# The end of the last block of a state-space and expert kernel: another order of the sums, and the last result accumulated on transposed sums in halves

## The chip, the cores and the metric

One Trainium2 chip, one core. The metric is the device time of one execution in microseconds (us): 611.15 is the median of three runs of the kernel before (610.99 to 611.33). Engines are named as the profile names them: PE is TensorE (PEld its weight loads), DVE is VectorE, ACT is ScalarE, POOL is GpSimd, SP is SyncE, which issues the DMAs here. A bank is one of the eight 128x512 fp32 accumulators of PSUM, the memory that PE writes.

## The reference

A chunked state-space block makes 3072 rows of 256 values; every row then goes through four experts, and the four outputs are added with the row's normalised weights. The change touches only the end of the second part:

```
p = domain_probs / (domain_probs.sum(-1, keepdims=True) + 1e-09)
out = zeros((3072, 256))
for e in range(4):
    h = maximum(x @ w1[e], 0.0)          # w1[e]: 256 x 1024
    out += p[:, e:e + 1] * (h @ w2[e])   # w2[e]: 1024 x 256
```

Everything is fp32.

## The kernel before

**Blocks and units.** The 3072 tokens are worked on in four blocks of six chunks of 128 tokens, that is three pairs of 256 tokens. Each block passes over the 16 slices of 256 hidden features in units of four slices, one expert to a unit. A unit has first products (w1; `fours_first`), gating on DVE, and second products (w2; `second`).

**Products.** In place of the 24 products that a unit's block matrices (w2 cut in four by two, tokens in three pairs) would take one by one, a fast scheme (`G`) takes 20, numbered 0 to 19. Their operands are sums of weight tiles on one side and sums of gated activations (`fours_right`, made by DVE) on the other. One product of the second kind multiplies a 256x128 weight by 256x256 activations: two fp32 matmuls of 128x128 by 128x256, which the profile shows as four matmul records and four weight loads. Its output has 128 model features as rows and 256 tokens as columns.

**Accumulators.** The 20 second products go to 16 accumulators of 128x256: twelve take one product each, and (1,6), (5,18), (2,19) and (3,17) take two each. Two accumulators share a bank; such a pair is a house. `visit` makes a house: ACT copies its sums so far from a tile of kind V (128x512, in SBUF) into a bank (`seed`, line 1035), PE adds the products (line 1021), ACT copies the bank back into V (line 1321). A house in `HELD` (last unit only) stays in its bank. `LATE` is the order of the houses in the last unit.

**Results.** `result` adds and subtracts accumulators in pairs of 128x256 on DVE (`sum_`, line 1372; where no operand is in a bank POOL may take it) until six results stand: half d of the model features (0 or 1) by pair n of the tokens (0 to 2). In the last block each result is written to a tile of its own, and `leave_last` takes it out: PE turns it with two 128x128 transposes into a bank (line 1437), DVE or ACT copies the bank to SBUF (line 1442), SP issues one DMA of 128 KB (line 1444). `LAST` is the order of the six results, and `TAILS` says how many second products come behind each one's turn.

**What sets the order.** PE's instructions go in the order of the list `line`, written by the code. All other engines' orders come from a planner (`Plan.run`): it has a cost for every piece of work (a product 0.863 us, a turn 0.35, a sum 0.34), walks through time, and gives each engine that is free the ready piece with the earliest due time (`latest`). The orders are fixed when the program is built; on the chip each engine goes through its queue in that order and waits where an input is not there.

**The end before.** The last unit's second products run in the order of accumulators 7 9, 15 10, 11 13, 4 8, 12 14, 0 16, (1,6) (5,18), (3,17), (2,19); the last two, which share a house, each have a bank of their own (`APART`). Turn (1,0) and turn (0,0) come ahead of (3,17), turn (0,1) ahead of (2,19), turns (1,1), (1,2), (0,2) at the end. Result (0,2) is (2,19) + 13, result (1,2) is (3,17) + 10.

Of the kernel before, what the change touches and what calls it, by code (L numbers as in the profile page):

```python
# [12 lines left out]
P = 128  # L13
# [6 lines left out]
D512, D256 = .60, .34  # L20
# [287 lines left out]
G = Scheme()  # L308
# [18 lines left out]
def house(*accs):  # L327
    return tuple(a if isinstance(a, tuple) else (a,) for a in accs)
# [1 line left out]

G.houses = (house(7, 9), house(15, 10), house((2, 19), (3, 17)), house(11, 13), house(12, 14),
            house(4, 8), house((1, 6), (5, 18)), house(0, 16))
LATE = (house(7, 9), house(15, 10), house(11, 13), house(4, 8), house(12, 14), house(0, 16),
        house((1, 6), (5, 18)), house((2, 19), (3, 17)))
HELD, APART = LATE[-3:], LATE[-1:]
TAILS = 4, 4, 2, 0, 0, 0
LAST = (1, 0), (0, 0), (0, 1), (1, 1), (1, 2), (0, 2)

B = Scheme()
B.rows, B.pairs = 2, 2  # L340
# [20 lines left out]
def kernel(  # L361
# [446 lines left out]
    def dma(fn, n=1, kb=256, **kw):  # L808
        return plan.add({"SP": ISSUE * n}, fn, lag=LANDING + kb / 190, kb=kb, pieces=n, **kw)
# [7 lines left out]
    def on(e):  # L817
        return {"DVE": nc.vector, "POOL": nc.gpsimd}[e]

    def value(kind, **kw):  # L820
        return Value(kind, **kw)
# [217 lines left out]
    def whole(v):  # L1039
        return v.t if v.kind == "bank" else flat(v)  # L1040
# [230 lines left out]
    def fours_right(h):  # L1271

        T = {0: h[0, 0], 3: h[3, 2], 4: h[3, 0], 6: h[0, 1], 7: h[1, 0], 12: h[2, 0], 18: h[2, 1],
             19: h[0, 2]}
        T[5] = combine(h[3, 0], h[3, 1], reuse=False)
        v = combine(h[3, 1], h[0, 1])
        T[8] = combine(v, h[3, 0], reuse=False)
        T[1] = combine(h[1, 1], h[1, 0])
        T[2] = combine(h[1, 0], h[1, 2], reuse=False)
        u = combine(h[1, 2], h[3, 2])  # L1280
        T[9] = combine(u, h[1, 0], reuse=False)
        T[15] = combine(T[1], h[2, 1], reuse=False)
        T[10] = combine(u, T[15])
        T[17] = combine(h[2, 0], h[2, 2], reuse=False)
        w = combine(h[2, 2], h[0, 2])
        T[14] = combine(w, h[2, 0], reuse=False)
        x = combine(h[0, 0], T[8], reuse=False)
        T[16] = combine(x, T[14])
        T[11] = combine(T[9], v, -1, reuse=v)
        T[13] = combine(w, T[15], -1)  # L1290
        return T
# [3 lines left out]
    def visit(k, house, terms, last=False, only=None):  # L1295
# [31 lines left out]
                hold=HOLD)  # L1327
        return seq

    def second(k, key, groups, houses, held=(), put={}):  # L1330

        seq = []
        for house in houses:
            terms = [
                (acc, weights[key, fbs, 2][0][r],
                 lambda r=r, fbs=fbs: weights[key, fbs, 2][1](r), T[r])
                for acc in house for r in put.get(acc, acc) for fbs, T in groups if r in T]
            for only in reversed(house) if house in held and house in APART else (None,):
                if terms:
                    seq += visit(k, house, terms, house in held, only)  # L1340
        return seq

    def plain_first(fb):
# [8 lines left out]
            for i in range(2)]  # L1352
        return seq, gated(b, gate_of(0, fb), 0)

    def result(k):

        scheme = blocks[k].scheme

        def acc(r):
            for house in scheme.houses:  # L1360
                if r in house:
                    v, i = kept.get((k, (r,)), kept.get((k, house))), house.index(r)
                    return v, lambda: whole(v)[:, i * FB:i * FB + FB]

        def piece(v, i):
            return v, lambda: v.t[:, i]

        def sum_(x, y, sign, o):

            vs = dict.fromkeys((x[0], y[0]))  # L1370
            engines = B256 if all(v.kind != "bank" for v in (*vs, o[0])) else {"DVE": D256}
            plan.add(engines, lambda e: (on(e).tensor_add if sign > 0 else on(e).tensor_sub)(  # L1372
                o[1](), x[1](), y[1]()), reads=[v for v in vs if v is not o[0]],
                two=all(v.kind != "bank" for v in vs), writes=[o[0]])

        A = {r[0]: acc(r) for h in scheme.houses for r in h}

        def into(r, x, y, sign=1):
            sum_(x, y, sign, A[r])

        into(9, A[9], A[10])
        into(14, A[14], A[13])
        into(7, A[7], A[9])
        into(7, A[7], A[15])
        into(4, A[4], A[8])
        into(4, A[4], A[9])
        into(4, A[4], A[11], -1)
        into(11, A[11], A[7], -1)
        into(13, A[13], A[7])
        into(12, A[12], A[14])  # L1390
        into(12, A[12], A[15])
        into(10, A[10], A[12])
        into(12, A[12], A[4])
        into(8, A[11], A[8], -1)
        into(8, A[8], A[14], -1)
        into(8, A[8], A[16])
        parts = {(0, 0): (0, 1, 8), (0, 1): (1, -1, 11), (0, 2): (2, 1, 13),
                 (1, 0): (16, -1, 12), (1, 1): (5, 1, 4), (1, 2): (3, 1, 10)}
        if k < len(blocks) - 1:
            for r, sign, x in parts.values():  # L1400
                into(r, A[r], A[x], sign)
            return [A[r][0] for r in (0, 1, 2)]
        O = {}
        for d, n in LAST:
            r, sign, x = parts[d, n]
            O[d, n] = value("V")
            sum_(A[r], A[x], sign, piece(O[d, n], 0))
        return O

    def leave(k, O, due):  # L1410
        for n in range(len(O)):
# [13 lines left out]
                                    in_=v[32 * x:32 * x + 32, d, c % 2 * 4:c % 2 * 4 + 4])  # L1425
                        dma(fn, 2, 150, reads=[ot], due=due)

    def leave_last(k, O, order):
        dst = out.rearrange("(q k p) (d m) -> d k p q m", q=NSEQ, p=P, d=2)
        tails = []  # L1430
        for x, (d, n) in enumerate(order):
            o, t, r = O[d, n], value("bank", fills=False), value("V")
            c = blocks[k].first + 2 * n

            def turn(e, o=o, t=t):
                for i in range(2):
                    nc.tensor.transpose(
                        t.t[:, i * P:i * P + P], o.t[:, 0, i * P:i * P + P], ident[:, 0])

            tails.append(plan.add({"PE": .35}, turn, reads=[o], writes=[t]))  # L1440
            copy = (nc.vector.tensor_copy, nc.scalar.copy)[x % 2]
            plan.add({("DVE", "ACT")[x % 2]: .36}, lambda e, t=t, r=r, copy=copy: copy(
                out=r.t[:, 0], in_=t.t[:, :2 * P]), reads=[t], writes=[r])
            dma(lambda e, c=c, d=d, r=r: nc.sync.dma_start(
                out=dst[d, c // NSEQ][:, c % NSEQ:c % NSEQ + 2],
                in_=r.t[:, 0].rearrange("p (q m) -> p q m", q=2)), kb=128, reads=[r])
        return tails

    def put(*seqs):
# [104 lines left out]
    for u, (k, fbs) in enumerate(units):  # L1556
        of_block = [v for v, (q, _) in enumerate(units) if q == k]
        i = u - of_block[0] + (not k)
        if u + 1 < len(units):
            unit_weights(u + 1)  # L1560
        if u == of_block[0] and k:
            token_sums(k, G, k)
        seq, h = fours_first(k, fbs)
        lead = 0 if u else LEAD
        merged = seq[:lead] + put(behind, seq[lead:])
        ends.append(merged[-1])
        if not u:
            fold()
        if ending is not None:
            leave(*ending, due=lambda n=u + AFTER: ends[min(n, len(ends) - 1)])  # L1570
            ending = None
        final = u == len(units) - 1
        behind = second(k, k, [(fbs, fours_right(h))], LATE if final else G.houses, HELD if final else ())
        if u == of_block[-1] and k < len(blocks) - 1:
            ending = k, result(k)

        at = {}
        if k < len(blocks) - 1:
            for unit, x, what in PAIRS_AT[k > 0]:
                if unit != i:  # L1580
                    continue
                cs = [blocks[k + 1].first + 2 * int(p) + j for p in what[1:] for j in range(2)]
                mark = len(line)
                if what[0] == "s":
                    for c in cs:
                        fetch(c)
                        decays(c)
                    scores(cs)
                else:
                    outputs(cs)  # L1590
                    for c in cs:
                        carry(c)
                at.setdefault(x, []).extend(line[mark:])
                del line[mark:]
        for x, w in enumerate(merged):
            line.extend(at.get(x, []))
            line.append(w)
    O = result(len(blocks) - 1)
    for i, w in enumerate(leave_last(len(blocks) - 1, O, LAST)):
        behind.insert(len(behind) - TAILS[i], w)  # L1600
    line.extend(behind)

    done = plan.run(line, now, {"PE": now, "DVE": now - 2.6, "ACT": now + .9, "POOL": now - 1.6,
# [56 lines left out]
```

## Time and profile before

| | |
|---|---|
| median of three runs | 611.15 us |
| the profiled execution: its time, its span | 612.22 us, 610.5 us |
| PE busy | 603.0 us, 99% of the span, 3385 records |
| DVE busy | 488.3 us, 80% |
| ACT busy | 296.6 us, 49% |
| POOL busy | 153.9 us, 25% |
| PE's share of the chain that ended last | 93% |
| granted clock of TensorE, mean | 0.999 |

The span runs from the first to the last instruction of the core; the execution's time has a little more around it. Busy time counts what an engine works, a matmul's end being modelled, so that the next matmul starts before the one ahead is shown to end: steps on PE are to be read from start to start. "The chain that ended last" is followed back from the last instruction, at each step to what released it. In a line such as `bank<-v,w 128*128 128x256 f32 x16` stand the output, the operands, the stationary tile's shape, the moving operand's shape and the number of records.

### The profile page before, as it was taken

What the parts mean: (1) busy time and instruction counts of PE and PEld (TensorE: products, weight loads), DVE (VectorE), ACT (ScalarE), POOL (GpSimd) and SP (SyncE); (2) the same over time, 40 slices, a digit from 0 to 9 for tenths busy, and PEclk for the clock granted to TensorE, in tenths of its full rate; (3) what the DMA queues carried; (4) which work ended last, traced back from release to release, by engine and by line L of the source; (5) the groups of instructions that cost most, each with busy time, mean ns of one, the idle gap of its engine ahead of it and who ended that gap; (6) DMA issues with size and microseconds to landing.
All of it is one profiled execution on the core that took longest, in us unless ns stands there. A gap on an engine that the chain in (4) does not pass through costs nothing.

```text
span 610.5 us, 10066 instructions
## 1 busy us (share of the span) xinstructions
PE 603.0 (99%) x3385; PEld 514.7 (84%) x3385; DVE 488.3 (80%) x843; ACT 296.6 (49%) x699; POOL 153.9 (25%) x204
## 2 busy tenths in 40 slices
PE   8999999999999999999999999999999999999997
PEld 5778878888888888888888888888888888888885
DVE  7779887999989894877979988396786989575775
ACT  5567465389443328948251334734444142434441
POOL 5656664536452002776200100200000000000000
PEclk9999999999999999999999999999999999999999
DMA  6866669787823239792422325962241332964001
GB/s 209 272 225 203 217 206 316 262 287 265 289 79 112 45 73 346 276 294 105 148 86 87 113 33 158 309 204 82 74 141 67 99 75 52 354 192 131 1 0 53
DMA packets 88548, 99.78 MB, mean 163 GB/s; under 512 B 26916, under 2 KB 54192, under 8 KB 88496
## 3 DMA queue, kind: packets, MB, share of 16 engines
q1 hardware_dynamic: 88340, 99.08, 51.4%
q8 instruction: 27, 0.44, 0.3%
q14 instruction: 25, 0.20, 0.1%
q10 hardware_dynamic: 156, 0.06, 0.0%
HBM read 78.93 MB, written 20.17 MB: 162 GB/s over the span
## 4 chain that ended last, share of the span: by engine, by line
PE 93%; DMA 2%; ACT 2%; DVE 1%; issue 0%; POOL 0%; SPq 0%; ACTq 0%; DVEq 0%; POOLq 0%
PE bank L1021 88%; PE bank L502 2%; PE bank L551 2%; DMA ah<-cum_d 1%; ACT A L561 1%; PE bank L967 1%; DMA ab<-cum_d 1%; PE bank L688 1%; DMA cum_d<-cum 1%; POOL w L1081 0%; ACT v L982 0%; DVE bank L1179 0%; ACT MT L526 0%; DVE LT L519 0%; DVE v L1372 0%
## 5 line engine op out<-in xcount | busy, mean ns | idle before, releaser
L1021 PE MATMUL bank<-v,w 128*128 128x256 f32 x1640 | 385.3, 380 | 0.0
L1021 PEld LDWEIGHTS bank<-v,w 128*128 128x128 f32 x1640 | 310.4, 190 | 45.3 <-issue 2.1
L1021 PE MATMUL bank<-Y,w 128*128 128x256 f32 x692 | 177.5, 381 | 0.8 <-ACT LT L982 0.4
L1021 PEld LDWEIGHTS bank<-Y,w 128*128 128x128 f32 x692 | 130.2, 190 | 22.2 <-issue 1.5
L1321 ACT COPY v<-bank 128x512 f32<-128x512 f32 x106 | 62.1, 585 | 173.9 <-PE bank L1021 172.9
L1048 DVE TENSOR_TENSOR v<-v,v 128x512 f32<-128x512 f32 x174 | 130.2, 760 | 1.3
L1056 DVE SCALAR_TENSOR_TENSOR v<-bank,gate 128x512 f32<-128x512 f32 x143 | 98.1, 686 | 36.2 <-PE bank L1021 32.4
L1081 POOL TENSOR_TENSOR w<-w,w 128x512 f32<-128x512 f32 (+1 forms) x74 | 80.2, 1094 | 55.1 <-DVE v L1048 15.1
L1030 ACT COPY v<-bank 128x512 f32<-128x512 f32 x99 | 57.9, 586 | 49.2 <-PE bank L1021 42.7
L1179 DVE TENSOR_TENSOR bank<-bank,v 128x512 f32<-128x512 f32 x79 | 53.7, 694 | 33.4 <-PE bank L1021 23.7
L1035 ACT COPY bank<-v 128x512 f32<-128x512 f32 x126 | 72.8, 594 | 10.6 <-DVE v L1056 7.3
L1021 PE MATMUL bank<-LT,w 128*128 128x256 f32 x228 | 58.0, 379 | 0.0
L526 ACT ACTIVATE MT<-ab,neg 128x128 f32<-128x128 f32 x160 | 50.3, 391 | 5.1 <-DMA ab<-cum_d 5.1
L1021 PEld LDWEIGHTS bank<-LT,w 128*128 128x128 f32 x228 | 43.2, 190 | 6.1 <-issue 0.3
L536 POOL TENSOR_SCALAR_AFFINE_SELECT MT<-MT 128x512 f32<-128x512 f32 x38 | 25.3, 675 | 74.7 <-ACT MT L526 56.7
L1048 DVE TENSOR_TENSOR v<-bank,v 128x512 f32<-128x512 f32 x29 | 19.9, 687 | 10.4 <-PE bank L1021 8.8
L944 DVE TENSOR_TENSOR MT<-bank,MT 128x512 f32<-128x512 f32 x36 | 22.7, 678 | 0.4 <-PE bank L502 0.4
L1321 ACT COPY LT<-bank 128x512 f32<-128x512 f32 x15 | 8.8, 586 | 27.8 <-PE bank L1021 24.9
L1056 DVE SCALAR_TENSOR_TENSOR v<-v,gate 128x512 f32<-128x512 f32 x29 | 20.3, 701 | 0.4
L1056 DVE SCALAR_TENSOR_TENSOR LT<-bank,gate 128x512 f32<-128x512 f32 x19 | 13.0, 686 | 7.4 <-PE bank L1021 7.0
L1372 DVE TENSOR_TENSOR v<-v,v 128x256 f32<-128x256 f32 x45 | 17.8, 417 | 1.1 <-ACT v L1321 0.7
L1048 DVE TENSOR_TENSOR v<-v,LT 128x512 f32<-128x512 f32 x25 | 16.9, 683 | 0.3
(128 smaller groups left out, 324.5 us busy)
## 6 DMA issues: line engine op xcount, KB each, us to landing
w<-w_d SPq DMA_DIRECT2D x128, 256.0 KB
w<-in_w_dram SPq DMA_DIRECT2D x72, 256.0 KB
w_d<-w SPq DMA_DIRECT2D x64, 256.0 KB
ab<-cum_d SPq DMA_DIRECT2D x20, 512.0 KB
gate<-p_d SPq DMA_DIRECT2D x15, 384.0 KB
xb<-in_xbc_dram SPq DMA_DIRECT2D x17, 192.0 KB
xb<-in_xbc_dram SPq DMA_DIRECT2D x7, 320.0 KB
out_dram<-v SPq DMA_DIRECT2D x112, 16.0 KB
```

What stands on the lines that cost most here:

```text
L526: nc.scalar.activation(out=MT[:, place(c, h), 0:P], in_=ab[:, h * P:h * P + P], func=AF.Exp, bias=neg[:, h % NT, NQ * real(c) + h // NT:NQ ...
L536: nc.gpsimd.affine_select(out=MT[:, h:h + n, 0:P], in_=MT[:, h:h + n, 0:P], compare_op=ALU.is_ge, fill=0.0, base=0, pattern=[[0, n], [1, P ...
L944: nc.vector.tensor_mul(to, g, to)
L1021: nc.tensor.matmul(out=o, lhsT=w[:, j], rhs=x if half is None else x[:, j], start=(start and j == 0), stop=(j == 1), skip_group_check=True)
L1030: act(.5, lambda e: nc.scalar.copy(out=flat(v), in_=bank.t), reads=[bank], writes=[v])
L1035: act(.54 if to - lo > FB else .32, lambda e: nc.scalar.copy(out=bank.t[:, lo:to], in_=flat(v)[:, lo:to]), reads=[v], writes=[bank])
L1048: plan.add(engines, lambda e: (on(e).tensor_add if sign > 0 else on(e).tensor_sub)(flat(v), whole(x), whole(y)), reads=[x, y], writes=[v], ...
L1056: dve(D512, lambda e: nc.vector.scalar_tensor_tensor(out=h.t, in0=whole(x).rearrange("p (j m) -> p j m", j=JJ), scalar=0.0, in1=g.t[:, 2 * ...
L1081: (on(e).tensor_add if sign > 0 else on(e).tensor_sub)(out, x, y)
L1179: dve(D512, lambda e: (nc.vector.tensor_add if sign > 0 else nc.vector.tensor_sub)(to.t, bank.t, whole(x)), reads=[x, bank], writes=[to])
L1321: act(.5, lambda e: nc.scalar.copy(out=flat(v), in_=bank.t), reads=[bank], writes=[v], hold=HOLD)
L1372: plan.add(engines, lambda e: (on(e).tensor_add if sign > 0 else on(e).tensor_sub)(o[1](), x[1](), y[1]()), reads=[v for v in vs if v is n ...
```

## The change

The houses of the last unit run in another order: 7 9, 15 10, 11 13, 4 8, (1,6) (5,18), 12 14, 0 16. The held houses are (1,6) (5,18), then 12 14, then 0 16. `second` and `result` lose what they had for the last unit and the last block, and `leave_last` goes; a new function `last` writes out the end of the last block:

- The sums are written in another order, with other intermediate values (one more tile, `q`). Results (0,1) and (1,1) come first, then (1,0), (0,0), (1,2); each is turned, copied and sent as before (`piece`), the copies alternating between ACT and DVE.
- (3,17) is made alone in half a bank, seeded from V, as before.
- (2,19) is not seeded. DVE adds its sums so far, in V, to accumulator 13; PE turns the two halves of this sum into two banks; and the products 2 and 19 are then added to these banks with the activations as the stationary operand, 128 tokens at a time, and the weights as the moving one: 128 tokens as rows, 128 features as columns. Behind each half comes a copy of 128x128 (ACT for the first, DVE for the second) and a DMA of 64 KB.
- `TAILS` puts turn (0,1) ahead of product 0, (1,1) ahead of 16, (1,0) and the two single transposes ahead of the first half, (0,0) between that half's products, (1,2) ahead of the second half.

```diff
-LATE = (house(7, 9), house(15, 10), house(11, 13), house(4, 8), house(12, 14), house(0, 16),
-        house((1, 6), (5, 18)), house((2, 19), (3, 17)))
-HELD, APART = LATE[-3:], LATE[-1:]
-TAILS = 4, 4, 2, 0, 0, 0
-LAST = (1, 0), (0, 0), (0, 1), (1, 1), (1, 2), (0, 2)
+LATE = (house(7, 9), house(15, 10), house(11, 13), house(4, 8), house((1, 6), (5, 18)),
+        house(12, 14), house(0, 16))
+HELD, APART = LATE[-3:], house((2, 19), (3, 17))
+TAILS = 8, 7, 4, 3, 2, 4, 4
...
-    def leave_last(k, O, order):
+    def last(k, groups):
+
+        seq = second(k, k, groups, LATE, HELD)
+        A = accumulators(k, LATE)
...
+        def turn(o, t, i, at):
+            nc.tensor.transpose(t.t[:, at:at + P], o[1]()[:, i * P:i * P + P], ident[:, 0])
+
+        def send(d, n, r, to):
             c = blocks[k].first + 2 * n
...
+            dma(lambda e: nc.sync.dma_start(
+                out=dst[d, c // NSEQ][:, c % NSEQ + to.start:c % NSEQ + to.stop],
+                in_=r.t[:, 0, to.start * P:to.stop * P].rearrange("p (q m) -> p q m", m=P)),
+                kb=64 * (to.stop - to.start), reads=[r])
+
+        def piece(d, n, x, y, sign):
+            o, t, r = fresh(), value("bank", fills=False), value("V")
+            sum_(x, y, sign, o)
+            tails.append(plan.add({"PE": .35}, lambda e: [turn(o, t, i, i * P) for i in range(2)],
+                                  reads=[o[0]], writes=[t]))
+            x = len(tails) % 2
+            copy = (nc.vector.tensor_copy, nc.scalar.copy)[x]
+            plan.add({("DVE", "ACT")[x]: .36}, lambda e: copy(
                 out=r.t[:, 0], in_=t.t[:, :2 * P]), reads=[t], writes=[r])
+            send(d, n, r, slice(0, 2))
+
+        into(9, 9, 10)
+        into(7, 7, 9)
+        into(7, 7, 15)
+        into(15, 15, 13)
+        into(9, 9, 11, -1)
+        into(11, 11, 7, -1)
+        q = A["q"] = fresh()
+        sum_(A[11], A[13], -1, q)
+        into(13, 13, 7)
+        into(10, 10, 15)
+        into(4, 4, 8)
+        into(4, 4, 9)
+        into(8, "q", 8, -1)
+        into(15, 15, 4)
+        piece(0, 1, A[1], A[11], -1)
+        piece(1, 1, A[5], A[4], 1)
+        into(15, 15, 12)
+        into(15, 15, 14)
+        into(8, 8, 14, -1)
+        piece(1, 0, A[16], A[15], -1)
+        into(8, 8, 16)
+        piece(0, 0, A[0], A[8], 1)
+
+        into(10, 10, 12)
+        into(10, 10, 14)
+        two, three = APART
+        terms = terms_of(k, groups, APART)
+        begun = kept[k, APART]
+        seq += visit(k, APART, terms, True, three)
+        third = kept[k, (three,)]
+        piece(1, 2, (third, lambda: whole(third)[:, FB:]), A[10], 1)
+        o, ends = fresh(), [value("bank", seeded=True) for _ in range(2)]
+        sum_((begun, lambda: flat(begun)[:, :FB]), A[13], 1, o)
+        tails.extend(plan.add({"PE": .2}, lambda e, t=t, i=i: turn(o, t, i, 0), reads=[o[0]], writes=[t])
+                     for i, t in enumerate(ends))
+        for i, t in enumerate(ends):
+            r = value("V")
+            for acc, w, view, x in terms:
...
+                def fn(e, i=i, t=t, view=view, x=x):
+                    for j in range(JJ):
+                        nc.tensor.matmul(
+                            out=t.t[:, :P], lhsT=x.t[:, j, i * P:i * P + P], rhs=view()[:, j],
+                            start=False, stop=j == JJ - 1, skip_group_check=True)
+
+                seq.append(plan.add({"PE": .52}, fn, reads=[w, x], writes=[t]))
+            plan.add({("ACT", "DVE")[i]: .25}, lambda e, i=i, t=t, r=r: (nc.scalar.copy, nc.vector.tensor_copy)[i](
+                out=r.t[:, 0, i * P:i * P + P], in_=t.t[:, :P]), reads=[t], writes=[r])
+            send(0, 2, r, slice(i, i + 1))
+        return [w for i, x in enumerate(seq)
+                for w in (*[t for t, n in zip(tails, TAILS) if n == len(seq) - i], x)]
...
-        behind = second(k, k, [(fbs, fours_right(h))], LATE if final else G.houses, HELD if final else ())
+        groups = [(fbs, fours_right(h))]
+        behind = last(k, groups) if final else second(k, k, groups, G.houses)
```

More of the change, by code (lines that the diff above doesn't have):

```diff
@@ L1328, in visit, with terms_of @@
         return seq
+    def terms_of(key, groups, house, put={}):
+        return [(acc, weights[key, fbs, 2][0][r],
+                 lambda r=r, fbs=fbs: weights[key, fbs, 2][1](r), T[r])
+                for acc in house for r in put.get(acc, acc) for fbs, T in groups if r in T]
     def second(k, key, groups, houses, held=(), put={}):
@@ L1333, in second @@
         for house in houses:
[L1334 to L1340, printed above, removed]
+            terms = terms_of(key, groups, house, put)
+            if terms:
+                seq += visit(k, house, terms, house in held)
         return seq
@@ L1353, in plain_first, with sum_, accumulators, acc @@
         return seq, gated(b, gate_of(0, fb), 0)
-    def result(k):
[L1357 to L1376, printed above, removed]
+    def sum_(x, y, sign, o):
+        vs = dict.fromkeys((x[0], y[0]))
+        engines = B256 if all(v.kind != "bank" for v in (*vs, o[0])) else {"DVE": D256}
+        plan.add(engines, lambda e: (on(e).tensor_add if sign > 0 else on(e).tensor_sub)(
+            o[1](), x[1](), y[1]()), reads=[v for v in vs if v is not o[0]],
+            two=all(v.kind != "bank" for v in vs), writes=[o[0]])
+    def accumulators(k, houses):
+        def acc(house, i):
+            v = kept[k, house]
+            return v, lambda: whole(v)[:, i * FB:i * FB + FB]
+        return {r[0]: acc(h, i) for h in houses for i, r in enumerate(h)}
+    def result(k):
+        A = accumulators(k, blocks[k].scheme.houses)
         def into(r, x, y, sign=1):
@@ L1398, in result @@
                  (1, 0): (16, -1, 12), (1, 1): (5, 1, 4), (1, 2): (3, 1, 10)}
[L1399 to L1408, printed above, removed]
+        for r, sign, x in parts.values():
+            into(r, A[r], A[x], sign)
+        return [A[r][0] for r in (0, 1, 2)]
     def leave(k, O, due):
@@ L1426, in leave @@
                         dma(fn, 2, 150, reads=[ot], due=due)
-    def leave_last(k, O, order):
+    def last(k, groups):
+        seq = second(k, k, groups, LATE, HELD)
+        A = accumulators(k, LATE)
         dst = out.rearrange("(q k p) (d m) -> d k p q m", q=NSEQ, p=P, d=2)
         tails = []
-        for x, (d, n) in enumerate(order):
-            o, t, r = O[d, n], value("bank", fills=False), value("V")
-            c = blocks[k].first + 2 * n
[L1435 to L1442, printed above, removed]
-                out=r.t[:, 0], in_=t.t[:, :2 * P]), reads=[t], writes=[r])
[L1444 to L1447, printed above, removed]
@@ new lines, in fresh, with into @@
+        def fresh():
+            v = value("V")
+            return v, lambda: v.t[:, 0]
+        def into(r, x, y, sign=1):
+            sum_(A[x], A[y], sign, A[r])
+        def turn(o, t, i, at):
+            nc.tensor.transpose(t.t[:, at:at + P], o[1]()[:, i * P:i * P + P], ident[:, 0])
+        def send(d, n, r, to):
+            c = blocks[k].first + 2 * n
+            dma(lambda e: nc.sync.dma_start(
+                out=dst[d, c // NSEQ][:, c % NSEQ + to.start:c % NSEQ + to.stop],
+                in_=r.t[:, 0, to.start * P:to.stop * P].rearrange("p (q m) -> p q m", m=P)),
+                kb=64 * (to.stop - to.start), reads=[r])
@@ new lines, in last @@
+        tails.extend(plan.add({"PE": .2}, lambda e, t=t, i=i: turn(o, t, i, 0), reads=[o[0]], writes=[t])
[3 more added lines that the diff above has]
+            for acc, w, view, x in terms:
+                if acc != two:
+                    continue
+                def fn(e, i=i, t=t, view=view, x=x):
[7 more added lines that the diff above has]
+            send(0, 2, r, slice(i, i + 1))
@@ L1597 @@
             line.append(w)
-    O = result(len(blocks) - 1)
-    for i, w in enumerate(leave_last(len(blocks) - 1, O, LAST)):
-        behind.insert(len(behind) - TAILS[i], w)
     line.extend(behind)
```

## The prediction

> **What bounds the kernel now.** I read the page first. In its table of engines PE is busy 603.0 of 610.5 us, and its chain is 93% PE. The table of waits gives PE few waits after the opening; one of them, 0.7 us for DVE at line 1437, lies at the end. So nearly everything up to 600 us is a gapless stream of products that the change leaves as it is, and only the last 20 us matter. For those I read the chain in order of time (start, length, what; x counts instructions):
>
> ```profile
> 600.95 0.77 DVE v L1372 x2
> 601.71 0.14 issue
> 601.85 0.41 PE bank L1437 x2
> 602.26 1.73 PE bank L1021 x8
> 603.99 0.22 PE bank L1437 x2
> 604.21 1.74 PE bank L1021 x8
> 605.95 0.02 issue
> 605.97 0.43 DVE v L1372
> 606.41 0.05 issue
> 606.45 0.45 PE bank L1437 x2
> 606.90 0.02 issue
> 606.93 0.37 ACT v L1442
> ```
>
> Two things are to be seen. Between 600.92 and 601.85 the chain leaves PE: two sums on DVE (line 1372) come ahead of a turn. And after the last product four steps follow each other: sum, turn, copy, transfer. The timeline of the sync engine and the stretches of the DMA engines (busy share, then GB/s, in the last two columns) show the transfer's end:
>
> ```profile
> 607.56 0.44 SPq L1444 DMA_DIRECT2D out_dram<-v  x1
> ```
> ```profile
> 607.40:607.60 0.20, 0.00 (x0) 0.00 (x0) 0.00 (x0) 0.00 (x0) 0.00 (x0) 1.00 0.43 131
> ...
> 608.80:609.00 0.20, 0.00 (x0) 0.00 (x0) 0.00 (x0) 0.00 (x0) 0.00 (x0) 0.79 0.92 274
> 609.00:609.20 0.20, 0.00 (x0) 0.00 (x0) 0.00 (x0) 0.00 (x0) 0.00 (x0) 0.50 0.14 36
> 609.20:609.40 0.20, 0.00 (x0) 0.00 (x0) 0.00 (x0) 0.00 (x0) 0.00 (x0) 0.50 0.00 0
> ```
>
> Three transfers of 128 KB are issued at 606.59, 607.06 and 607.56, one every 0.48 us. The last copy is done at 607.30, so the third issue also waits 0.26 us for its queue. Bytes flow from about 607.5 to 609.05: 0.9 us after an issue, then 0.52 us per 128 KB. From the last byte to the end of the span it is 1.45 us.
>
> **The change, part by part.** Times are on the span of the profiled execution (610.5 us; that execution took 612.22, 1.07 over the median of 611.15, so I carry the difference over to the median). PE steps are taken from start to start, since ends are modelled.
>
> 1. *PE up to the last product.* The last unit's second products start at 586.93, and 16 of them end at 600.75: 0.864 each (four records). In before follow a turn (0.22), then 0.88 of standing still until 601.85, a turn (0.25), two products (to 603.82), a turn (0.22) and two products, to 605.77. The standing still is the order of DVE's queue: the sum at 600.95 waited 0.42 us for PE's bank (the products of 1, 6, 5, 18), and behind it stood the sum for turn (0,0), whose inputs were ready at 600.53. In the new order the last products are 1 6 5 18, 12, 14, 0, 16, 3, 17, and each turn comes at least one product's length after the sum it needs could run (worked out in step 2). So PE has 18 products (15.54), five turns of two transposes at 0.22 (1.10), two single transposes (0.22), and the narrow products.
>
> 2. *The sums.* DVE now has 25 sums (22 before) of 0.42 us; independent ones start 0.36 apart (six in 2.22), dependent ones 0.46. (7,9) to (4,8) keep their place and their ACT evacuation (0.585, starting 0.20 after the bank). From 591.2, sums 1 to 3 run; from 592.9, six; the four behind (4,8) end near 597.1. The bank of 1 and 5 is ready at 586.93 + 12 x 0.864 + 0.2 = 597.5, so the sums for (0,1) and (1,1) end at 597.9 and 598.3, ahead of their turns at 599.0 and 600.1. The bank (12,14) is ready at 599.2: five sums and one copy occupy DVE until about 601.7. Bank (0,16) is ready at 601.4; the sum for (1,0) ends near 602.15, that for (0,0) near 602.9. Their turns are due at 602.92 and 603.83: 0.8 and 0.9 to spare. That for (1,2) runs 603.1 to 603.5, due at 604.5. The sum under the last accumulator needs only a V tile and 13, ready by 596. Behind a late sum every later DVE sum is queued, and PE's whole list behind the turn; with the slacks above I count nothing. If that cover goes, each microsecond beyond 0.8 goes to the end.
>
> 3. *The narrow products.* Accumulator (2,19) is made in two halves of 128 tokens: 8 matmuls of 128 columns, 16 records, in place of 8 records of 256 columns (1.73). The program has matmuls of just that form in its opening (line 726); in the second group of them PE starts the next line's work right behind:
>
> ```profile
> 14.60 2.05 PE L726 MATMUL bank<-v,w 128*128 128x128 f32 x16
> 16.48 3.62 PE L1021 MATMUL bank<-v,w 128*128 128x256 f32 x16
> ```
> ```profile
> 14.59 1.86 PEld L726 LDWEIGHTS bank<-v,w 128*128 128x128 f32 x16 [0.44 <-ACT v L792]
> ```
>
> 16 records take 16.48 - 14.60 = 1.88 us, 0.1175 each, though one weight load shows 0.19. I take 1.88: 0.15 more than the wide form. The bounds are 1.73 (columns alone) and 16 x 0.19 = 3.04 (each load by itself).
>
> PE's list then: 601.19 after 16 products and two turns; 602.92 after 3 and 17; 603.36 after a turn and the two single transposes; 603.83 half of the first half; 604.05 turn (0,0); 604.52; 604.74 turn (1,2); 605.68 the end of issue. Against 605.77 that is -0.09: 0.91 of standing still and its restart go, 0.67 of turns moved ahead of the last product and 0.15 of narrowness come.
>
> 4. *Behind the last product.* Before: 605.77 to the last issue at 607.56, 1.79. After: 0.20 to DVE, as at 605.97, a DVE copy of 128x128, and 0.03 to the issue (copy ends 606.56, issue 606.59). That copy is not in the trace; DVE's copy of 128x256 is 0.414, ACT's copies of 128x256 and 128x128 from a bank are 0.372 and 0.266, so I take 0.28, from 0.20 (DVE's smallest tile row here, 128x32) to 0.41. Together 0.51: issue at 606.19, if the queue is free. It has to be: (0,0) is turned at 603.83, copied at 604.25 and issued at 604.70; the first half goes at 605.18, (1,2) at 605.66, the next slot is 606.14. That is just in time; each issue that comes late puts up to 0.1 to 0.3 on the end. Gain 1.37 with step 3.
>
> 5. *The last transfer* is 64 KB in place of 128: 0.26 for 0.52 us, gain 0.26; between nothing and 0.35 (no queue ahead of it). The tail of 1.45 stays. The Trainium skill (DMA: Bandwidth & Descriptors, Anatomy of one DMA) gives each transfer a fixed part of about 2.0 us, most of it the wait for the write to be confirmed, and bytes at 436 GB/s; the trace's 0.9 + 1.45 us agrees roughly with the first, while its 0.52 us per 128 KB is about 250 GB/s. By the page's rate this step would give 0.15 and the sum 1.52.
>
> 6. *Nothing counted:* one seed of half a bank less on ACT (0.38), one evacuation less (0.585), both on an engine that idles before nearly every instruction here. The order of the last unit's right-hand sums on DVE may shift, since 1, 6, 5, 18 are due 3.5 us earlier; the last such sum ends at 591.0 and 1 is due at 593.8, so PE should not see it. Weights: DMA moved 1 and 0 GB/s in the page's two slices (15 us each) ahead of the last one, so no load is late. From -0.2 to +0.5 for all of this.
>
> Sum: 1.37 + 0.26 = 1.63, from 610.5 to 608.9 on the span, and **609.5** on the median.
>
> **Rivals.** What can be told from no change in this kernel is 0.2%, 1.22 us.
>
> - *PE still waits at a turn.* For it: this is what before shows, 0.88 us, from a sum queued behind another that waited for a bank; DVE has three more sums and slacks of 0.8. Against: in the new order no sum that waits for a late bank stands ahead of one that is due sooner. A wait of the old size gives 609.5 + 0.9 = 610.4, no change. Chance 0.16.
> - *The weight loads set the pace of the narrow products*, 0.19 per record: +1.16, 610.7, no change. Against it the 0.1175 above. Chance 0.07.
> - *The loads don't overlap at all* when the records are narrow: 0.19 + 0.1175 each, 4.92 in place of 1.88, +3.04 and 612.5, slower. It decides once a record costs over 0.30 us (1.63 + 1.22 + 1.88 = 4.73 for 16). Against it stand the loads of line 726, 16 in 1.86 us where one lasts 0.19: they lie over each other and over the matmuls. Only another state of the tiles (the activations are now the weights, and cut out of a 256-wide tile) could change that. Chance 0.05. The Trainium skill (TensorE: Matmul & The Clock Gate, Part 3, The mechanism) says that a weight load overlaps matmuls in flight only when its row group differs, which all 128 rows here never do; that would be this case. The 64 loads of the last 16 products start 0.216 apart with 0.19 each, without stretching the matmuls, so the trace does not agree.
> - *The change does not do what it says:* (1,2) or the first half is late, and both halves leave together. The last issue is then one slot later, 0.5: 610.0, at the edge of no change. Chance 0.05; another 0.02 is for a disturbance of the stages ahead that makes it slower.
>
> The forecast, all steps within their bounds (609.0 to 609.9), has 0.65. **Faster** by over 0.2% (under 609.93) is the forecast and a part of the late turn (a wait under 0.4) and of the late issue, 0.71; **within** 0.2% 0.22; **slower** 0.07. The range from 608.9 (step 5 at its best, the copy at 0.20, -0.2 from step 6, 0.2 for the measurement) to 610.6 leaves out about 0.15.
>
> **What would show it.** After: no gap on PE between the start of the second products and its last record, which belongs to a narrow product and ends about 18.9 us after that start; 16 narrow records in about 1.9 us; behind them one copy of 128x128, one issue about 0.5 us after PE's last start, 64 KB, and the end about 2.6 us later. If PE stops ahead of a turn, step 2 is wrong; if the narrow records stand 0.19 apart or more, step 3; if the last issue touches the one before it, step 4; if the second products start at another time than 586.9, step 6.

## The result and the profile after

The changed kernel takes 610.38 us (median of 16 runs), the kernel before 611.7 us in runs beside them (16 runs). The ratio is 0.9977, 95% interval 0.9968 to 0.9986: 1.4 us faster, between 0.9 and 2.0. The forecast was 1.63 us. The profiled execution of the changed kernel has a span of 607.8 us, 2.7 less than the one of before; 1.0 of these 2.7 us lies ahead of the end that the change rewrites (below). The forecast was a gain of over 0.2%; the measured one is 0.23%, and its interval, 0.14 to 0.32%, holds that line inside it.

The chain of the changed kernel in order of time (start, length, what) answers the one shown of before:

```profile
599.48 2.59 PE bank L1020 x12
602.07 0.44 PE bank L1434 x4
602.51 0.45 PE bank L1497 x4
602.95 0.23 PE bank L1434 x2
603.19 0.45 PE bank L1497 x4
603.63 0.22 PE bank L1434 x2
603.85 0.91 PE bank L1497 x8
604.76 0.02 issue
604.78 0.29 DVE v L1502
```

The chain no longer leaves PE until the last product is done: the two DVE sums ahead of a turn are gone. Line 1434 is the turns, line 1497 the narrow products: 4, 4 and 8 records in 0.45, 0.45 and 0.91 us, 1.81 in all, 0.113 each. Behind them stands one step, a copy of 128x128, in place of sum, turn and copy.

The timelines of DVE and SP and the stretches of the DMA engines (last two columns: busy share, GB/s) show the end:

```profile
604.78 0.29 DVE L1502 COPY v<-bank 128x128 f32<-128x128 f32 x1 [1.07 <-PE bank L1497]
```
```profile
605.21 0.42 SPq L1438 DMA_DIRECT2D out_dram<-v  x1
```
```profile
606.20:606.40 0.20, 0.00 (x0) 0.00 (x0) 0.00 (x0) 0.00 (x0) 0.00 (x0) 1.00 0.89 261
606.40:606.60 0.20, 0.00 (x0) 0.00 (x0) 0.00 (x0) 0.00 (x0) 0.00 (x0) 1.00 0.08 21
606.60:607.00 0.40, 0.00 (x0) 0.00 (x0) 0.00 (x0) 0.00 (x0) 0.00 (x0) 1.00 0.00 0
```

The copy is done at 605.07, the last issue starts at 605.21, the last bytes have moved by about 606.4, and the span ends at 607.8. From the last issue to the end it is 2.59 us, where it was 2.94.

**A measure that leaves the opening out.** In the two profiles the last unit's second products start at 586.93 and at 585.92 (before, then after; the third line is the last of PE's list after the change):

```profile
586.93 13.98 PE L1021 MATMUL bank<-v,w 128*128 128x256 f32 x64
```
```profile
585.92 12.25 PE L1020 MATMUL bank<-v,w 128*128 128x256 f32 x56
603.69 1.06 PE L1497 MATMUL bank<-w,v 128*128 128x128 f32 x8
```

The products, turns and sums that the change puts in another order lie behind this start, so I compare the stretch from there to the span's end: 23.57 us before, 21.88 after, 1.69 less. The table holds all profiles; the ratio is that of the times to the kernel before, measured beside each run. One of the twelve executions of the change run again took 1630.9 us and is not counted.

| kernel | second products start | span | stretch | against before | ratio (95%) |
|---|---|---|---|---|---|
| before | 586.93 | 610.5 | 23.57 | | |
| the change | 585.92 | 607.8 | 21.88 | -1.69 | 0.9977 (0.9968 to 0.9986) |
| the change again | 589.03 | 611.1 | 22.07 | -1.50 | 0.9976 (0.9964 to 0.9987) |
| one turn later | 586.69 | 609.3 | 22.61 | -0.96 | 0.9984 (0.9975 to 0.9993) |
| sum first | 587.36 | 610.2 | 22.84 | -0.73 | 0.9988 (0.9974 to 1.0001) |
| order only | 585.98 | 608.8 | 22.82 | -0.75 | 0.9988 (0.9979 to 0.9997) |
| halves only | 586.31 | 608.9 | 22.59 | -0.98 | 0.9983 (0.9974 to 0.9992) |
| one transfer | 586.38 | 608.4 | 22.02 | -1.55 | 0.9976 (0.9967 to 0.9985) |
| turns earlier | 586.52 | 608.2 | 21.68 | -1.89 | 0.9968 (0.9956 to 0.9980) |

A ratio of 0.999 is 0.61 us. In each row the ratio and the stretch tell the same to within 0.3 us, so nothing outside the stretch is needed to explain the times. Each stretch comes from one profile, and the two profiles of the changed kernel differ by 0.19 us: a smaller difference between two rows is not shown by them.

### The profile page after: what moved, and what is told of

Its sections match the earlier page's. It is cut to its first block, busy times and chain, and to the rows that moved or that the text cites. A ratio compares the mean times of both kernels' runs of the same rounds, so it can differ in the third digit from the quotient of the medians.

```text
span 607.8 us, 10091 instructions
## 1 busy us (share of the span) xinstructions
PE 602.5 (99%) x3393; PEld 515.4 (85%) x3393; DVE 489.5 (81%) x846; ACT 295.8 (49%) x698; POOL 155.0 (25%) x204
## 4 chain that ended last, share of the span: by engine, by line
PE 97%; ACT 1%; DVE 1%; issue 0%; POOL 0%
PE bank L1020 90%; PE bank L550 2%; PE bank L501 2%; PE bank L687 1%; PE bank L966 1%; PE bank L725 1%; ACT A L560 1%; PE bank L662 0%; PE bank L1497 0%; PE bank L1434 0%; DVE bank L1178 0%; POOL w L1080 0%; DVE LT L518 0%; DVE v L1047 0%; ACT v L981 0%
```

## The experiments

The theory: the end is a chain whose parts add up, and the change shortens it in two independent ways, by the order (PE does not stand still ahead of a turn, and fewer turns come behind the last product) and by the narrow products on transposed sums (sum and turn leave the end, the last copy and transfer are halved). The rivals: the order alone does it, the halves alone do it, or the gain lies elsewhere.

### One turn later in the kernel before

```diff
-TAILS = 4, 4, 2, 0, 0, 0
+TAILS = 4, 2, 2, 0, 0, 0
```

> The kernel before with one constant changed: TAILS = 4, 2, 2, 0, 0, 0, so that turn (0,0) comes behind the two products 3 and 17 instead of ahead of them. The measure is the stretch from the start of the last unit's second products to the end of the span: 23.57 us before (586.93 to 610.5), 21.88 after the change (585.92 to 607.8). My theory: PE's 0.88 us of standing still ahead of turn (0,0) were on the path, so they go in full: 22.7, ratio to before 0.9985. Rival A, the wait was hidden by the end's own chain (sums, sync queue): 23.5, ratio 1.000. Rival B, the wait moves to another turn: between 22.9 and 23.5.

Measured: 22.61, ratio 0.9984. The chain of this kernel:

```profile
600.66 0.22 PE bank L1437 x2
600.88 1.73 PE bank L1021 x8
602.61 0.44 PE bank L1437 x4
603.05 1.74 PE bank L1021 x8
604.79 0.02 issue
```

PE goes from turn (1,0) at 600.66 straight into the products; the two turns behind them run without a gap. The stretch falls by 0.96. PE's list up to the last product gives 0.92 of it (17.92 us for 18.84): the 0.88 of standing still and the slower step of the turn behind it. The rest lies behind the last issue, 2.89 us for 2.94. So the gap was on the path in full, and one constant would have brought over half of what the change brings.

### The sum first in the kernel before

The sums for the other results are made to stand behind that for (0,0) in the planner, which moves it ahead in DVE's queue. The diff shows the core; `sum_` also hands the new argument to the planner:

```diff
...
-            sum_(A[r], A[x], sign, piece(O[d, n], 0))
+            w = sum_(A[r], A[x], sign, piece(O[d, n], 0), behind=ahead)
+            if (d, n) == (0, 0):
+                ahead = [w]
```

> The kernel before, with only DVE's queue changed: in the planner the sums for (0,1), (1,1), (1,2) and (0,2) stand behind the sum for (0,0), so DVE does not wait for the bank of 1 and 5 ahead of it. Turns and products keep their places. My theory: the 0.88 us of standing still ahead of turn (0,0) came from that order alone; now the sum ends at about 601.0 in the time of the first profile and PE stands still for 0.1 to 0.15: stretch 22.8, ratio to before 0.9988. Rival A, DVE's chain of sums itself is late: 23.5, no change. Rival B, the sums pushed back now hold up a later turn: 23.0 to 23.5.

Measured: 22.84, ratio 0.9988; its interval reaches 1.0001, so the times alone can't tell it from no change, and the profile decides. Before, DVE's queue had three sums in a row, the first held up 0.42 us by PE's bank and that for (0,0) behind it; now the sum for (0,0) comes first and alone:

```profile
600.95 1.09 DVE L1372 TENSOR_TENSOR v<-bank,v 128x256 f32<-128x256 f32 x3 [0.42 <-PE bank L1021]
```
```profile
600.99 0.42 DVE L1372 TENSOR_TENSOR v<-bank,v 128x256 f32<-128x256 f32 x1
```

Turns, products and their places are those of before; PE's timeline has

```profile
601.17 0.38 PE L1439 MATMUL bank<-ident,LT 128*128 128x128 f32 x2
601.55 0.41 PE L1439 MATMUL bank<-ident,v 128*128 128x128 f32 x2
601.80 1.03 PE L1021 MATMUL bank<-LT,w 128*128 128x256 f32 x4
```

The second turn starts 0.38 behind the first one, which takes 0.22, so 0.16 of waiting is left of 0.88, and PE's list up to the last product is 0.72 shorter (18.12 us for 18.84). The wait came from the order of DVE's queue: the sum at its head waited for a bank of PE's while the sum that PE needed next was ready behind it.

### The order alone

The changed kernel, but (2,19) as before: seeded, two wide products, sum, turn, copy, one transfer (the diff shows the core).

```diff
-        o, ends = fresh(), [value("bank", seeded=True) for _ in range(2)]
...
+        seq += visit(k, APART, terms, True, two)
+        second_ = kept[k, (two,)]
+        piece(0, 2, (second_, lambda: whole(second_)[:, :FB]), A[13], 1)
```

with `TAILS = 6, 5, 2, 1, 1, 0`.

> The changed kernel with its new order of houses, sums and turns, but (2,19) made the old way: its sums are seeded into half a bank, two products of 256 columns, then sum, turn, copy and one transfer of 128 KB. My theory: PE needs 20 x 0.864 + 5 x 0.22 = 18.4 us to the end of the products (18.84 before), then 1.16 to the copy, 0.41 copy, 0.03 to the issue, 1.49 + 1.45 to the end: stretch 22.9, ratio to before 0.9989. Rival A, the order is all that the change brings: 21.9, ratio 0.9977. Rival B, the order brings nothing without the halves: 23.6.

Measured: 22.82, ratio 0.9988. The chain's end:

```profile
603.64 0.88 PE bank L1020 x4
604.52 0.02 issue
604.54 0.43 DVE v L1360
604.98 0.04 issue
605.02 0.45 PE bank L1434 x2
605.48 0.02 issue
605.50 0.42 DVE v L1450
```

The last product, sum, turn and copy follow each other as before, but the last issue, at 605.95, no longer queues behind two others.

### The halves alone

The order of houses and sums of the kernel before, and only the last accumulator made as in the change. It is written as an edit of the changed kernel, whose list of sums (not shown) is put back to the order of before:

```diff
-LATE = (house(7, 9), house(15, 10), house(11, 13), house(4, 8), house((1, 6), (5, 18)),
-        house(12, 14), house(0, 16))
-HELD, APART = LATE[-3:], house((2, 19), (3, 17))
-TAILS = 8, 7, 4, 3, 2, 4, 4
+LATE = (house(7, 9), house(15, 10), house(11, 13), house(4, 8), house(12, 14), house(0, 16),
+        house((1, 6), (5, 18)))
+HELD, APART = LATE[-2:], house((2, 19), (3, 17))
+TAILS = 6, 6, 4, 4, 2, 4, 4
...
```

(turns (1,0) and (0,0) ahead of 3 and 17, as before; (0,1), (1,1) and the two single transposes ahead of the first half, (1,2) ahead of the second).

> The kernel before with its own order of houses and sums, but (2,19) accumulated as in the change, on transposed sums in two halves of 128 tokens; turns (1,0) and (0,0) ahead of 3 and 17 as before, (0,1), (1,1) and the two single transposes ahead of the first half, (1,2) ahead of the second. My theory: the 0.88 us ahead of turn (0,0) stay, the end behind the last product shrinks as in the change: PE 19.65, then 0.20 + 0.29 + 0.03 to the last issue and 2.6 to the end: stretch 22.8, ratio to before 0.9988. Rival A, the halves bring all: 21.9. Rival B, the halves bring nothing by themselves (narrow products, two more transposes, one more issue eat it): 23.5, ratio 1.000.

Measured: 22.59, ratio 0.9983. The chain has the gap of before and the end of the change:

```profile
600.33 0.77 DVE v L1360 x2
601.09 0.14 issue
601.23 0.41 PE bank L1434 x2
...
605.13 0.91 PE bank L1492 x8
606.04 0.02 issue
606.06 0.29 DVE v L1497
```

Order alone brings 0.75, halves alone 0.98: 1.73 together, against 1.69 and 1.50 for both at once in the two profiles of the changed kernel. The parts add up to within the difference of those two, and both rivals fall by the stretches: each part alone falls short of the whole. The times agree, but their intervals (0.9979 to 0.9997, 0.9974 to 0.9992, 0.9968 to 0.9986 for both) overlap, so they don't decide it. The halves brought 0.2 more than I had expected: the end behind the last issue (2.52 us from 606.38, expected 2.6) and PE's list (19.57 us, expected 19.65).

### One transfer

The two halves are copied into one tile, which leaves in one transfer of 128 KB:

```diff
-                out=r.t[:, 0, i * P:i * P + P], in_=t.t[:, :P]), reads=[t], writes=[r])
-            send(0, 2, r, slice(i, i + 1))
+                out=r.t[:, 0, i * P:i * P + P], in_=t.t[:, :P]), reads=[t], part=[r])
+        send(0, 2, r, slice(0, 2))
```

> The changed kernel, but the two halves of (2,19) are copied into one tile and leave in one transfer of 128 KB behind the second copy, not in two of 64 KB. My theory: the last issue comes about 0.1 us earlier (one transfer less in the sync queue) and its bytes take 0.26 us longer: stretch 22.05, ratio to the changed kernel 1.0003, which the times can't tell, so the profile decides. Rival A, the size of the last transfer does not count, only its fixed part: 21.8. Rival B, a transfer of 128 KB behind another one queues: 22.3 or more.

Measured: 22.02, 0.14 more than the first profile of the change and 0.05 less than the second; the times are the same (0.9976). The last issue, at 605.56, comes 0.03 behind its copy, and its bytes keep the DMA engines busy for 0.44 us in the rows below, twice the 0.22 us of the last 64 KB in the kernel with the turns earlier (further down):

```profile
606.40:606.60 0.20, 0.00 (x0) 0.00 (x0) 0.00 (x0) 0.00 (x0) 0.00 (x0) 1.00 0.61 184
606.60:606.80 0.20, 0.00 (x0) 0.00 (x0) 0.00 (x0) 0.00 (x0) 0.00 (x0) 1.00 0.98 297
606.80:607.00 0.20, 0.00 (x0) 0.00 (x0) 0.00 (x0) 0.00 (x0) 0.00 (x0) 1.00 0.61 174
```

By this profile and the first one of the change a half transfer is worth 0.14 and not 0.26, since it costs one more slot of the sync queue: its last issue comes 0.11 later behind the start of the second products (19.29 us, here 19.18). But 0.14 is within what the two profiles of the changed kernel differ by (0.19), so that the last transfer's halving pays at all is not shown.

### The change again, and turns earlier

> The changed kernel again, beside the runs above on one chip, to see how much of the 2.7 us between the two first profiles is chance of the opening: in those profiles the second products of the last unit started 1.01 us earlier after the change, and 1.69 us lay behind that start. My theory: the stretch is 21.9 again to within 0.1, while the start of the second products moves freely by some tenths to 1 us, and the ratio to before is about 0.997. Rival, the change also makes the part ahead shorter: the start stays near 585.9, 1 us earlier than in kernels with the end of before.

Measured: stretch 22.07, ratio 0.9976. The stretch came out 0.19 longer than the first time, more than I had expected. PE's part is the same (18.67 us to the last product's end of issue, 18.68 the first time); the difference is the issue of the first half, which took SP 0.62 us where others take 0.34 to 0.44, and so pushed the two behind it:

```profile
607.32 0.62 SPq L1438 DMA_DIRECT2D out_dram<-v  x1
```

The copy ended at 608.18, the last issue started at 608.51. The second products started at 589.03, against 585.92 in the first profile of the same program, so the start moves by up to 3 us with nothing changed. This start alone does not refute the rival: the four other kernels with the narrow products or the new order started between 585.98 and 586.52, ahead of all three with the end of before (586.69 to 587.36). Two other things speak against it. From 40 to 580 us PE's busy time is the same in all nine profiles to within 0.03 us, so that the start is set in the first 40 us, far from the change; of the 1.01 us between the first two profiles, 0.87 is time that PE stood idle longer in the first 30 us of the one of before. And a part ahead that is 1 us shorter would make the changed kernel 2.7 us faster, where the times say 0.9 to 2.0. So most of the 1.01 us is chance of the opening; that the change moves the opening by some tenths is not excluded.

The other kernel frees that queue:

```diff
-TAILS = 8, 7, 4, 3, 2, 4, 4
+TAILS = 8, 7, 4, 4, 3, 4, 4
```

> The changed kernel with TAILS = 8, 7, 4, 4, 3, 4, 4: turn (0,0) ahead of the first half and turn (1,2) ahead of that half's second product, one product's length earlier each. In the changed kernel the last copy ended at 605.07 and the last issue came at 605.21, right behind another issue, with (1,2)'s 128 KB still on their way. My theory: the earlier turns free the sync queue and the DMA engines, the last issue comes 0.03 behind its copy and its bytes flow at once: 0.1 to 0.3 off the stretch, 21.6 to 21.8 after 21.88; PE's list stays 18.7 long. Rival A: the last issue and its bytes are paced by something else, 21.9. Rival B: one of the turns now comes ahead of its sum and PE waits: 22.0 or more.

Measured: 21.68, ratio to before 0.9968 (0.9956 to 0.9980), median 609.89 of five runs beside 609.83 of eleven for the change on the same chip. The last issue now starts at 605.68, 0.03 behind its copy (605.36 + 0.29):

```profile
605.68 0.34 SPq L1438 DMA_DIRECT2D out_dram<-v  x1
```

PE's list is as long as in the change and has no gap. The issue behind its copy came as expected. By its stretch this is the shortest of all these kernels, by 0.20 and 0.39 under the two profiles of the change; by the times it is faster than before, but no difference from the change is shown.

## Why the prediction was right

The direction, the size and the mechanism were right: 1.63 us forecast, 1.69 and 1.50 in the stretch of two profiles, 1.4 (0.9 to 2.0) in the times. The median of 610.38 lies 0.9 above the 609.5 on record, inside the range; most of that is the base: the three runs shown had a median of 611.15, the 16 runs beside the change 611.7. The line of 0.2% for "faster" was met by the point, 0.23%, and not by the whole interval (0.14 to 0.32%). By step:

1. **PE up to the last product.** Right: no gap, and the list from the start of the second products to the last record's start plus its step is 18.68 us, forecast 18.75. That the gap came from DVE's order and was on the path in full was argued, and is now shown by two kernels of before (0.96 and 0.73 gained by moving a turn or a sum alone).
2. **The sums.** Right: those for (1,0), (0,0), (1,2) ended 1.1, 1.0 and 0.8 us ahead of their turns (600.80, 601.80, 602.65 against 601.90, 602.79, 603.47); forecast 0.8, 0.9, 1.0. DVE made only three of the five sums on bank (12,14) ahead of the one for (1,0), and the other two behind it, so the order within the queue was not quite the one forecast.
3. **The narrow products.** 1.81 us, forecast 1.88 from the opening's records; the bound of 0.19 per record, and the rival that loads don't overlap, are refuted by the step of 0.113 per record, and by the weight loads themselves, on PE's load queue:

```profile
603.58 0.97 PEld L1497 LDWEIGHTS bank<-w,v 128*128 128x128 f32 x8
```

Eight loads of 0.19 us each fit into 0.97. The Trainium skill's rule that loads overlap only with another row group (TensorE: Matmul & The Clock Gate, Part 3, The mechanism) does not hold for these loads of all 128 rows: they run from 603.58 to 604.55, under the matmuls that start from 603.69 on.

4. **Behind the last product.** Here the forecast was 0.1 short: 0.61 from PE's last step to the issue, forecast 0.51. The copy of 128x128 took 0.29 (0.28), but the issue came 0.14 behind its end: the issues ahead of it started at 604.21 and 604.72, one every 0.5 us, and its slot, which step 4 called "just in time", was that much late. That is the sign which the prediction had named for an error in step 4. In the kernel with the turns earlier the issue comes 0.03 behind its copy.
5. **The last transfer.** 0.35 less from issue to end, the upper bound that was given; forecast 0.26. From the last byte to the end it was about 1.4 us, forecast 1.45. In the one direct comparison (one transfer of 128 KB, from 605.56) it is 2.84 against 2.59, 0.25: the size that the trace's own rate gives. The 0.15 by the other rate in step 5 is too small; the fit that the prediction takes from the Trainium skill (DMA: Bandwidth & Descriptors, Anatomy of one DMA) is given there for transfers that GpSimd issues, and these are issued by SP.
6. **Nothing counted** for the part ahead: nothing in the times speaks against it, since ratio and stretch agree to within 0.3 us. The sign that the prediction had named, another start of the second products than 586.9, did come (585.92), but was badly chosen: that start moves by 3 us between two profiles of one program.

PE's list was 0.07 shorter than forecast, step 4 0.10 longer, step 5 0.09 shorter. That they add up to within 0.06 is in part luck.

## What to carry to other kernels

At the end of a kernel that one engine fills, read the chain from the last product on: every step behind it counts in full, and linear steps (adding earlier sums, turning) can often be moved ahead of the last product by accumulating onto their result. An engine's queue that is ordered by a plan can put an instruction that waits ahead of one that is due; a gap on the critical engine, while the queue of another stands still with due work behind its head, is the sign. Here moving the consumer or the waiting work gained 0.96 and 0.73 us, about as much as the larger rewrite with its halves (0.98). When the last step is halved, count the issues ahead of it: here a slot of 0.5 us in the sync queue held up a transfer whose halving saves 0.25.

## What the runs showed of the hardware

The chance in these profiles sits in the first 40 us: from there to 580 us PE's busy time is the same in all nine to within 0.03 us (539.21 to 539.24 of 540 us), at a clock of 1.00. In the profile of the change run again, PE stood still longer in the opening and then lost clock. Its stretches (PE's busy time, granted clock, DMA share, GB/s) are

```profile
25.00:30.00 5.00, 4.08 (x46) 1.00 0.82 203
30.00:40.00 10.00, 9.93 (x87) 0.83 0.93 306
```

and the same program's first profile has 5.00 and 10.00 us busy at clock 1.00 there. Of the 3.1 us between the two, 0.5 is idle time in the first 10 us, 0.9 the gap between 25 and 30 us (PE waits there once, 0.9 us, for a copy by ACT), and 10 x 0.17 = 1.7 the clock granted behind it. Another profile (the sum first) has a gap of 0.9 us at the same place and a clock of 1.00 behind it, so the gap alone does not explain the lower clock; what does stays open.
